# Low parts of the fp32 split moved from GpSimd to VectorE in the last two token tiles and the second feed-forward layer

## The chip, the cores and the metric

The kernel runs on one core of one Trainium2 chip. The metric is device time in microseconds, the median of several runs. The engines are PE (TensorE matmul, with PEld for its weight loads), DVE (VectorE), ACT (ScalarE), POOL (GpSimd) and SP (SyncE, which here issues all DMAs). They run side by side, each in the order of its own instruction queue, and wait for each other by semaphores.

## The reference, cut to what matters

Three stages are computed one after the other on 3072 tokens (4 batches of 768). All data are fp32.

```
# 1. linear attention with decay, 8 heads of 32, state 16, in chunks along the sequence
y = scan_attention(x, a, B, C)            # [3072 tokens, 256]
# 2. first feed-forward layer, w1 w2 w3: 256 x 768, w_out: 768 x 256
h = max(max(y @ w1, y @ w2), y @ w3)
x = h @ w_out
# 3. second feed-forward layer, w_gate w_val: 256 x 1536, w_out: 1536 x 256
out = (sigmoid(x @ w_gate) * (x @ w_val)) @ w_out
```

## The kernel before, in words

**Split in high and low parts.** Each fp32 operand of a big matmul is kept as two tiles of the faster type float32r: `hi` is a rounded copy made by ACT, `lo = value - hi` is what rounding lost. A product is three matmuls: lo times hi, hi times lo, hi times hi. So every weight block, every input operand and every gated tile needs one ACT cast and one subtraction, and a low part can't be made before its cast.

**Stages.** Tokens are cut in six tiles of 512 (t = 0 to 5). Attention chunks are computed ahead of and between the matmuls of the first layer in tiles 0 to 3. In the first layer a tile has six blocks m of 128 hidden columns. A block, called a layer step below, is 18 matmuls into three PSUM banks (tiles `u_t_m_0` to `u_t_m_2`) and 6 matmuls of the down product (tiles `o_t_0`, `o_t_1`) of the block before it. The three PSUM banks are a ring: matmuls of the next step can only write bank 1 after the bank of this step has been read.

**What is done with a step's banks** (function `most`): ACT copies bank 0 to `s` (L467), DVE takes the maximum with bank 1 (L469) and with bank 2 (L471), ACT casts `s` to `hi` (L460), and a subtraction makes `lo` (L462, in `hidden`).

**Weights of the second layer** come as raw 64-bit words in 18 pieces (`g0`, `v0`, `d0` to `g5`, `v5`, `d5`) and are decoded on the chip by `decode`: three ACT passes (L164, L169, L173), two DVE passes (L177, L182), for pieces g and v four small DVE sums (L195), ACT casts (L201), and the low parts (L204: one subtraction of 512 columns for the four blocks, and for g and v another of 384 columns for three sums). Decoding starts in tile 4, one piece in a layer step, and goes on in the second layer. `behind(k)` is a hint on order: the instruction is issued after the last eviction of a PSUM bank on ACT (k = 0) or DVE (k = 1).

**Operands of the second layer.** `operands(p)` makes seven sums and differences of two token tiles and splits each (`operand`: L431 is the ACT cast, L432 the subtraction). p = 0 is made in tiles 4 and 5, p = 1 and 2 later. The second layer computes, for each p and each j of 6 pieces, 14 products of three matmuls (L605), evicts and gates them (L609 to L619, L670), splits the gated tile (L673 on ACT, L674 on DVE) and multiplies it by the down weights (L634).

**Order.** The program is written as generators that are advanced in turns; a scheduler then orders the instructions of each engine by its own estimate of time. So the place of an instruction on its engine is set by that scheduler, under the data dependences and the `behind` hints. All DMAs are issued by SP.

Of the kernel before, what the change touches and what calls it, by code (L numbers as in the profile page):

```python
# [8 lines left out]
F32 = mybir.dt.float32  # L9
# [6 lines left out]
ALU = mybir.AluOpType  # L16
# [10 lines left out]
NTT = NT // TT  # L27
# [43 lines left out]
def scan_attention_then_ffn(ctx: ExitStack, tc: tile.TileContext, xh, ah, bch, pick, bn, w1, w2, w3,  # L71
                            wo1, wg, wv, wo2, out):
    nc = tc.nc
    act, dve, pool, pe, sp = nc.scalar, nc.vector, nc.gpsimd, nc.tensor, nc.sync
# [41 lines left out]
    def store2(wpool, tags, name):  # L116

        nb = 4 if name[0] == "d" else 7
        if len(tags) == 1:
            w = wpool.tile([128, 2, nb, 128], F32R, tag=tags[0], name=f"w_{name}")  # L120
            hi, lo = w[:, 0], w[:, 1]
        else:
            hi, lo = (wpool.tile([128, nb, 128], F32R, tag=g, name=f"w_{name}{k}")
                      for k, g in enumerate(tags))
        wt2[name] = [(hi[:, b], lo[:, b]) for b in range(nb)]
        return hi, lo
# [25 lines left out]
    def decode(raw, wpool, blocks, name):  # L152
        nb = raw.shape[1]
        second = name[0] != "a"

        def behind(k):
            return tc.issue_after(evict[k].ins) if second else ExitStack()

        f1 = raw[..., 1]
        r = stp.tile([128, DEC // 128, 128], I32, tag="r", bufs=3, name=f"r_{name}")[:, 0:nb]  # L160
        sg = sgs[len(blocks_done) % len(sgs)][:, 0:nb]
        blocks_done.append(name)
        with behind(0):
            act.activation(out=sg.bitcast(F16).rearrange("p b (n t) -> p b n t", t=2)[..., 1], in_=f1.bitcast(F32),  # L164
                           func=AF.Identity, scale=2.0 ** -112)
        if second:
            yield
        with behind(0):
            act.mul(f1.bitcast(F32), f1.bitcast(F32), 2.0 ** -112)  # L169
        if second:  # L170
            yield
        with behind(0):
            act.mul(r, raw[..., 0].bitcast(U32), 2.0 ** -29)  # L173
        yield
        t = stp.tile([128, DEC // 128, 128], I32, tag="t", bufs=2, name=f"t_{name}")[:, 0:nb]
        with behind(1):
            dve.scalar_tensor_tensor(out=t, in0=f1, scalar=3, in1=sg, op0=ALU.logical_shift_left,  # L177
                                     op1=ALU.bitwise_or)
        if second:
            yield  # L180
        with behind(1):
            dve.tensor_tensor(out=r, in0=t, in1=r, op=ALU.add)  # L182
        yield
        if second:
            hi, lo = store2(wpool, blocks, name)
            parts = [(r.bitcast(F32), slice(0, 4))]
            if name[0] != "d":
                v = r.bitcast(F32)
                q = wq[0].tile([128, 3, 128], F32, tag="q", name=f"q_{name}")
                for k, (out, x, y, op) in enumerate(((q[:, 0], v[:, 1], v[:, 3], ALU.add),  # L190
                                                     (q[:, 2], v[:, 0], v[:, 1], ALU.subtract),
                                                     (q[:, 1], q[:, 0], v[:, 0], ALU.subtract),
                                                     (v[:, 1], v[:, 2], q[:, 1], ALU.subtract))):
                    with behind(1):
                        dve.tensor_tensor(out=out, in0=x, in1=y, op=op)  # L195
                    if k % 2:
                        yield
                parts.append((q, slice(4, 7)))
            for x, at in parts:
                with behind(0):  # L200
                    act.copy(hi[:, at], x)  # L201
                yield
            for x, at in parts:
                pool.tensor_tensor(out=lo[:, at], in0=x, in1=hi[:, at].bitcast(F32), op=ALU.subtract)  # L204
            return
        w = wpool.tile([128, 2, nb, 128], F32R, tag=name, name=f"w_{name}")
        blocks += [(w[:, 0, b], w[:, 1, b]) for b in range(nb)]
        act.copy(w[:, 0], r.bitcast(F32))
        yield
        pool.tensor_tensor(out=w[:, 1], in0=r.bitcast(F32), in1=w[:, 0].bitcast(F32),  # L210
                           op=ALU.subtract)

    def weights_tick(last=True):
        if loaded and last:
            pipe.add(decode(*loaded.pop(0)))
# [179 lines left out]
    def three(ps, ks, kn, w, blk, a_hi, a_lo):  # L395

        for k in ks:
            whi, wlo = w[blk(k)]
            pe.matmul(ps, wlo, a_hi(k), start=k == 0, stop=False)  # L399
            pe.matmul(ps, whi, a_lo(k), start=False, stop=False)  # L400
            pe.matmul(ps, whi, a_hi(k), start=False, stop=k == kn - 1)  # L401
# [18 lines left out]
    def at(k, t):  # L420
        return y1[:, k, t * TT:(t + 1) * TT]
# [8 lines left out]
    def operand(i, src, eng):  # L430
        act.copy(x7[0][:, SLOT[i]], src)  # L431
        eng.tensor_tensor(out=x7[1][:, SLOT[i]], in0=src, in1=x7[0][:, SLOT[i]].bitcast(F32),  # L432
                          op=ALU.subtract)

    def operands(p):

        eng = dve if p else pool
        b11, b12, b21, b22 = (at(k, 2 * p + t) for k in range(2) for t in range(2))
        operand(1, b11, eng)
        dve.tensor_tensor(out=b12, in0=b12, in1=b11, op=ALU.subtract)  # L440
        yield
        operand(2, b21, eng)
        yield
        operand(5, b12, eng)
        yield
        dve.tensor_tensor(out=b12, in0=b22, in1=b12, op=ALU.subtract)
        operand(6, b12, eng)
        yield
        dve.tensor_tensor(out=b11, in0=b12, in1=b11, op=ALU.subtract)
        operand(7, b11, eng)  # L450
        yield
        dve.tensor_tensor(out=b21, in0=b21, in1=b12, op=ALU.subtract)
        yield
        operand(3, b22, dve)
        yield
        operand(4, b21, dve)

    def hidden(s, hl, eng):
        yield
        act.copy(hl[0], s)  # L460
        yield
        eng.tensor_tensor(out=hl[1], in0=s, in1=hl[0].bitcast(F32), op=ALU.subtract)  # L462

    def most(s, banks, hl):

        yield
        evict[0] = act.copy(s, banks[0])  # L467
        yield
        dve.tensor_tensor(out=s, in0=banks[1], in1=s, op=ALU.max)  # L469
        yield  # L470
        evict[1] = dve.tensor_tensor(out=s, in0=banks[2], in1=s, op=ALU.max)  # L471
        yield from hidden(s, hl, pool)

    chain = Pipe()

# [4 lines left out]
    def layer(t, m, w, n, stages):  # L480

        o = (t * TT) % RING
        s = tmpp.tile([128, TT], F32, tag="s", bufs=3, name=f"s{n}_{t}_{m}")
        hl = [tmpp.tile([128, TT], F32R, tag=h, name=f"{h}{n}_{t}_{m}") for h in ("hi", "lo")]
        banks = []
        for j in range(n):
            ps = psu.tile([128, TT], F32, tag="up", name=f"u{n}_{t}_{m}_{j}")
            three(ps, range(KD), KD, w, lambda k: KD * j + k,
                  lambda k: xt_hi[:, k, o:o + TT], lambda k: xt_lo[:, k, o:o + TT])
            banks.append(ps)  # L490
            if j == 0:
                chain.add(stages(s, banks, hl))
            yield hl


# [151 lines left out]
    for p in range(NTT // 2):  # L647
        for j in range(M2 // 2):
            two = {k: Product(p, j, k) for k in "gv"}
            made = {}  # L650
            if p < 2 and j == M2 // 2 - 1:
                later = operands(p + 1)
            else:
                later = None
            for u, step in enumerate(PLAN):
# [8 lines left out]
                else:  # L664
                    kind, i = step[0], int(step[1])
                    k = two[kind].multiply(i)
                    if kind == "v" and k is not None:
# [7 lines left out]
                                          op=ALU.subtract)  # L675
# [76 lines left out]
```

## Time and profile before

| | |
|---|---|
| median of 3 runs | 569.61 us (568.42 to 570.89) |
| the profiled execution | 568.34 us |
| its span from first to last instruction | 566.2 us |
| mean granted TensorE clock | 0.985 |
| busy share of the span: PE, DVE, ACT, POOL | 94%, 70%, 57%, 33% |
| POOL instructions | 206 |

The span is 2.1 us shorter than the time of the same execution. A busy share is a mean over stages that have different limits: here attention lies in the first 200 us, tiles 4 and 5 of the first layer between about 213 and 285 us, the second layer behind them.

### The profile page before, as it was taken

How to read it: one execution, taken by the hardware profiler on the slowest of the kernel's cores; microseconds unless marked ns; L12 is line 12 of the kernel's file. 1: busy time of each engine (PE TensorE's matmuls, PEld its weight loads, DVE VectorE, ACT ScalarE, POOL GpSimd, SP SyncE). 2: the span in 40 equal slices, each digit the busy share in tenths (PEclk: the TensorE clock that was granted, in tenths of full speed). 3: DMA queues.
4: the chain of work that ended last, by engine and by line, in shares of the span. 5: the costliest groups of instructions: out<-in, count | busy, mean ns of one | idle time of the engine just before them, and what ended most of it. 6: DMA issues, size and time to landing. Idle time of an engine off the chain costs nothing.

```text
span 566.2 us, 7999 instructions
## 1 busy us (share of the span) xinstructions
PE 533.4 (94%) x2885; PEld 421.3 (74%) x2885; DVE 395.4 (70%) x603; ACT 325.0 (57%) x580; POOL 189.5 (33%) x206
## 2 busy tenths in 40 slices
PE   4768899999999999998989999999999999999996
PEld 4656667677777778876867877877888887788885
DVE  3899985666876733899987897586555567555555
ACT  4787735334434233667688887566555565555553
POOL 3567956464655433488641233000000000000000
PEclk9869899999999999999999999999999999999999
DMA  7999985893996119013220000002000002000001
GB/s 244 346 264 236 242 175 113 190 178 123 194 204 124 30 37 335 1 37 113 75 75 1 1 1 2 0 0 75 0 1 0 2 1 75 0 1 0 1 1 74
DMA packets 32007, 50.52 MB, mean 89 GB/s; under 512 B 3168, under 2 KB 17888, under 8 KB 31968
## 3 DMA queue, kind: packets, MB, share of 16 engines
q1 hardware_dynamic: 31968, 50.02, 33.8%
q8 instruction: 22, 0.36, 0.3%
q14 instruction: 17, 0.14, 0.1%
HBM read 38.51 MB, written 3.25 MB: 74 GB/s over the span
## 4 chain that ended last, share of the span: by engine, by line
PE 65%; DVE 14%; ACT 7%; DMA 7%; issue 4%; POOL 1%; SPq 1%; DVEq 0%; ACTq 0%; POOLq 0%
PE o L634 14%; PE ug L605 12%; PE uv L605 12%; PE u L399 6%; PE u L400 6%; PE u L401 6%; DMA raw_a<-in_w 3%; PE o L399 2%; PE y L350 2%; PE o L400 2%; PE o L401 2%; PE s L332 1%; DVE q_v L195 1%; DVE r_v L182 1%; DMA dec<-ad 1%
## 5 line engine op out<-in xcount | busy, mean ns | idle before, releaser
L634 PE MATMUL o<-hi,w_d 128*128 128x512 f32 x288 | 97.7, 390 | 0.6 <-ACT hi L673 0.6
L399 PE MATMUL u<-xt_hi,w_a 128*128 128x512 f32 x216 | 89.5, 414 | 6.2 <-DVE s L469 3.3
L605 PE MATMUL ug<-xt_hi,w_g 128*128 128x512 f32 x252 | 91.5, 391 | 1.4 <-ACT y L609 1.4
L605 PE MATMUL uv<-xt_hi,w_v 128*128 128x512 f32 x252 | 90.5, 391 | 0.5 <-DVE s L471 0.5
L400 PE MATMUL u<-xt_lo,w_a 128*128 128x512 f32 x216 | 85.9, 398 | 1.8 <-DVE xt_lo L361 1.8
L401 PE MATMUL u<-xt_hi,w_a 128*128 128x512 f32 x216 | 85.8, 397 | 0.0
L462 POOL TENSOR_TENSOR lo<-s,hi 128x512 fp32r<-128x512 f32 x36 | 50.6, 1404 | 42.1 <-ACT hi L460 41.9
L634 PEld LDWEIGHTS o<-hi,w_d 128*128 128x128 f32 x288 | 53.9, 188 | 12.3 <-ACT hi L673 1.3
L674 DVE TENSOR_TENSOR lo<-y,hi 128x512 fp32r<-128x512 f32 x72 | 50.8, 706 | 16.8 <-ACT hi L673 15.9
L288 DVE TENSOR_TENSOR_SCAN dec<-dec,delta 128x388 f32<-128x388 f32 x64 | 57.9, 945 | 2.3 <-DMA dec<-ad 2.1
L634 PE MATMUL o<-lo,w_d 128*128 128x512 f32 x144 | 56.6, 393 | 1.8 <-DVE lo L674 1.6
L605 PEld LDWEIGHTS ug<-xt_hi,w_g 128*128 128x128 f32 x252 | 47.3, 188 | 12.9 <-ACT y L609 1.8
L605 PEld LDWEIGHTS uv<-xt_hi,w_v 128*128 128x128 f32 x252 | 47.3, 188 | 11.9 <-DVE s L471 0.9
L460 ACT CAST hi<-s 128x512 fp32r<-128x512 f32 x36 | 22.3, 620 | 58.7 <-DVE s L471 58.4
L399 PEld LDWEIGHTS u<-xt_hi,w_a 128*128 128x128 f32 x216 | 41.5, 192 | 18.6 <-DVE s L469 4.1
L605 PE MATMUL ug<-xt_lo,w_g 128*128 128x512 f32 x126 | 49.1, 390 | 0.0
L605 PE MATMUL uv<-xt_lo,w_v 128*128 128x512 f32 x126 | 49.1, 389 | 0.0
L400 PEld LDWEIGHTS u<-xt_lo,w_a 128*128 128x128 f32 x216 | 41.5, 192 | 10.0 <-DVE xt_lo L361 2.3
L673 ACT CAST hi<-y 128x512 fp32r<-128x512 f32 x72 | 44.7, 621 | 6.7 <-DVE y L670 6.7
L401 PEld LDWEIGHTS u<-xt_hi,w_a 128*128 128x128 f32 x216 | 41.3, 191 | 9.2
L670 DVE TENSOR_TENSOR y<-uv,y 128x512 f32<-128x512 f32 x36 | 24.8, 688 | 32.9 <-PE uv L605 32.9
L612 DVE TENSOR_TENSOR y<-ug,y 128x512 f32<-128x512 f32 x36 | 24.8, 689 | 26.5 <-ACT y L609 18.9
(100 smaller groups left out, 987.0 us busy)
## 6 DMA issues: line engine op xcount, KB each, us to landing
dec<-ad SPq DMA_DIRECT2D x30, 388.0 KB, 5.6
raw_a<-in_w SPq DMA_DIRECT2D x18, 256.0 KB, 6.8
bi<-parts SPq DMA_DIRECT2D x36, 128.0 KB, 6.0
cs<-parts SPq DMA_DIRECT2D x36, 96.0 KB, 6.1
xs<-in_xh SPq DMA_DIRECT2D x6, 512.0 KB, 5.2
raw_g<-in_wg SPq DMA_DIRECT2D x6, 512.0 KB, 5.0
raw_v<-in_wv SPq DMA_DIRECT2D x6, 512.0 KB, 5.9
raw_d<-in_wo SPq DMA_DIRECT2D x6, 512.0 KB, 3.7
```

Source lines behind the costliest of these rows:

```text
L288: dve.tensor_tensor_scan(out=f, data0=f, data1=delta.rearrange("p u w -> p (u w)"), initial=0.0, op0=ALU.mult, op1=ALU.add)
L399: pe.matmul(ps, wlo, a_hi(k), start=k == 0, stop=False)
L400: pe.matmul(ps, whi, a_lo(k), start=False, stop=False)
L401: pe.matmul(ps, whi, a_hi(k), start=False, stop=k == kn - 1)
L460: act.copy(hl[0], s)
L462: eng.tensor_tensor(out=hl[1], in0=s, in1=hl[0].bitcast(F32), op=ALU.subtract)
L605: pe.matmul(ps, w, x, start=new and e == 0, stop=e == 2, skip_group_check=not new)
L612: evict[1] = dve.tensor_tensor(out=self.t[k], in0=ps, in1=self.t[k], op=ALU.add)
L634: pe.matmul(acc2[t][d], w, x, start=n == 1 and e == 0, stop=n == M2 and e == 2)
L670: evict[1] = dve.tensor_tensor(out=g, in0=v, in1=g, op=ALU.mult)
L673: act.copy(hl[0], g)
L674: dve.tensor_tensor(out=hl[1], in0=g, in1=hl[0].bitcast(F32), op=ALU.subtract)
```

## The change

Three subtractions that make low parts are given to DVE instead of POOL: those of the second layer's weights (L204, with the hint to stand behind the last eviction on DVE), those of the first five operands of `operands(0)` (L432; the later ones were on DVE already), and those of the hidden tiles of the first layer in token tiles 4 and 5 (L462). From the fifth tile on POOL does no arithmetic. No DMA, no matmul and no ACT instruction is added or taken away, and POOL issues no DMA in either kernel.

```
             for x, at in parts:
-                pool.tensor_tensor(out=lo[:, at], in0=x, in1=hi[:, at].bitcast(F32), op=ALU.subtract)
+                with behind(1):
+                    dve.tensor_tensor(out=lo[:, at], in0=x, in1=hi[:, at].bitcast(F32),
+                                      op=ALU.subtract)
...
     def operands(p):
-        eng = dve if p else pool
+        eng = dve
...
-    def most(s, banks, hl):
+    def most(s, banks, hl, eng):
...
-        yield from hidden(s, hl, pool)
+        yield from hidden(s, hl, eng)
...
-                chain.add(stages(s, banks, hl))
+                chain.add(stages(s, banks, hl, dve if t > NTT - 3 else pool))
```

Lines behind the first edit have numbers higher by two in the changed kernel (L471 there is L469 here). In the rows below `s_5_0` is the hidden tile of token tile 5, block 0, and `u_5_0_1` its PSUM bank 1; `y_91` holds token tiles.

DVE between the last maximum of step 4_5 and that of step 5_0, before:

```order
L471 TENSOR_TENSOR s_4_5_2528<-u_4_5_2_2557,s_4_5_2528 128x512
L177 SCALAR_TENSOR_TENSOR t_g_2574<-raw_g_2333,sg_88 128x512
L182 ISA r_g_2541<-t_g_2574,r_g_2541 128x1024
L195 TENSOR_TENSOR q_g_2600<-r_g_2541 128x128 x2
L195 TENSOR_TENSOR q_g_2600<-q_g_2600,r_g_2541 128x128
L195 TENSOR_TENSOR r_g_2541<-r_g_2541,q_g_2600 128x128
L446 TENSOR_TENSOR y_91<-y_91 128x512
L449 TENSOR_TENSOR y_91<-y_91 128x512
L469 TENSOR_TENSOR s_5_0_2576<-u_5_0_1_2590,s_5_0_2576 128x512
L452 TENSOR_TENSOR y_91<-y_91 128x512
L471 TENSOR_TENSOR s_5_0_2576<-u_5_0_2_2604,s_5_0_2576 128x512
```

The same place on DVE now (without the first maximum, which is still ahead of it):

```order
L177 SCALAR_TENSOR_TENSOR t_g_2574<-raw_g_2333,sg_88 128x512
L434 TENSOR_TENSOR xt_lo<-y_91,xt_hi 128x512 x2
L182 ISA r_g_2541<-t_g_2574,r_g_2541 128x1024
L464 TENSOR_TENSOR lo_4_5_2530<-s_4_5_2528,hi_4_5_2529 128x512
L448 TENSOR_TENSOR y_91<-y_91 128x512
L195 TENSOR_TENSOR q_g_2600<-r_g_2541 128x128 x2
L471 TENSOR_TENSOR s_5_0_2576<-u_5_0_1_2590,s_5_0_2576 128x512
L451 TENSOR_TENSOR y_91<-y_91 128x512
L454 TENSOR_TENSOR y_91<-y_91 128x512
L195 TENSOR_TENSOR q_g_2600<-q_g_2600,r_g_2541 128x128
L434 TENSOR_TENSOR xt_lo<-y_91,xt_hi 128x512
L473 TENSOR_TENSOR s_5_0_2576<-u_5_0_2_2604,s_5_0_2576 128x512
```

Four low parts (three operands, one hidden tile) stand in this stretch that stood on POOL, and the maximum of bank 1 is now ahead of part of the sums of piece g.

ACT at the passage from the first layer to the second, before (`ug`, `uv` are product banks of the second layer, `o_5` the down product of tile 5):

```order
L607 COPY uv_0_1_2931<-uv_0_0_2927 128x512
L619 ACT_TABLE_LOAD
L619 ACTIVATE y_91<-ug_0_1_2922 128x512
L201 CAST w_v_2936<-q_v_2937 128x384
L201 CAST w_v_2936<-r_v_2856 128x512
L609 COPY y_91<-ug_0_0_2918 128x512
L418 COPY y_91<-o_5_0_2669 128x512
L418 COPY y_91<-o_5_1_2670 128x512
L609 COPY sv_0_1_2973<-uv_0_0_2927 128x512
L673 CAST hi_0_0_2966<-y_91 128x512
```

And now:

```order
L609 COPY uv_0_1_2931<-uv_0_0_2927 128x512
L621 ACT_TABLE_LOAD
L621 ACTIVATE y_91<-ug_0_1_2922 128x512
L611 COPY y_91<-ug_0_0_2918 128x512
L611 COPY sv_0_1_2973<-uv_0_0_2927 128x512
L420 COPY y_91<-o_5_0_2669 128x512
L675 CAST hi_0_0_2966<-y_91 128x512
L201 CAST w_v_2936<-q_v_2937 128x384
L420 COPY y_91<-o_5_1_2670 128x512
L201 CAST w_v_2936<-r_v_2856 128x512
```

The first copy of a gate bank (L609 before) has moved ahead of the two casts of a weight piece.

## Rows read from the trace of the kernel before

**Rows 1.** Busy time of each engine in four stretches; columns in the first line.

```profile
core 0: us, PE busy (x) PEld busy (x) DVE busy (x) ACT busy (x) POOL busy (x), PEclk, DMA share, GB/s
200.00:229.30 29.30, 29.30 (x163) 23.61 (x162) 9.96 (x14) 10.89 (x19) 8.64 (x7) 1.00 0.50 180
229.30:250.00 20.70, 20.70 (x93) 17.15 (x92) 19.18 (x25) 15.45 (x27) 15.01 (x11) 1.00 0.00 0
250.00:297.00 47.00, 41.79 (x179) 32.52 (x178) 43.20 (x59) 33.03 (x60) 30.30 (x22) 1.00 0.28 90
297.00:352.00 55.00, 54.10 (x235) 43.47 (x234) 46.48 (x77) 46.38 (x86) 16.69 (x12) 1.00 0.00 1
```

**Rows 2.** Timeline of PE, matmuls with a wait: start, duration, [idle before, releaser].

```profile
254.55 0.50 PE L399 MATMUL u<-xt_hi,w_a 128*128 128x512 f32 x1 [1.33 <-DVE s L469]
...
261.66 0.50 PE L399 MATMUL u<-xt_hi,w_a 128*128 128x512 f32 x1 [1.96 <-DVE s L469]
...
284.45 0.50 PE L605 MATMUL uv<-xt_hi,w_v 128*128 128x512 f32 x1 [0.50 <-DVE s L471]
...
291.74 0.50 PE L605 MATMUL ug<-xt_hi,w_g 128*128 128x512 f32 x1 [1.39 <-ACT y L609]
```

**Rows 3.** Timeline of DVE, 239 to 299 us.

```profile
239.54 0.69 DVE L469 TENSOR_TENSOR s<-u,s 128x512 f32<-128x512 f32 x1
...
240.94 1.80 DVE L177 SCALAR_TENSOR_TENSOR t_d<-raw_d,sg 128x512 int32<-128x512 int32 x1
242.88 1.58 DVE L182 CUSTOM_DVE_ANT_0 r_d<-t_d,r_d 128x1024 uint16<-128x1024 uint16 x1
...
260.93 0.68 DVE L469 TENSOR_TENSOR s<-u,s 128x512 f32<-128x512 f32 x1
...
281.98 0.49 DVE L195 TENSOR_TENSOR q_g<-r_g 128x128 f32<-128x128 f32 x2
282.39 0.28 DVE L195 TENSOR_TENSOR q_g<-q_g,r_g 128x128 f32<-128x128 f32 x1
...
297.60 0.68 DVE L612 TENSOR_TENSOR y<-ug,y 128x512 f32<-128x512 f32 x1
298.20 0.68 DVE L182 CUSTOM_DVE_ANT_0 r_d<-t_d,r_d 128x1024 uint16<-128x1024 uint16 x1
```

**Rows 4.** Timeline of POOL beside them.

```profile
240.90 1.29 POOL L204 TENSOR_TENSOR w_v<-r_v,w_v 128x512 fp32r<-128x512 f32 x1
242.15 1.75 POOL L462 TENSOR_TENSOR lo<-s,hi 128x512 fp32r<-128x512 f32 x1
...
300.17 1.30 POOL L204 TENSOR_TENSOR w_d<-r_d,w_d 128x512 fp32r<-128x512 f32 x1 [7.16 <-ACT w_d L201]
```

**Rows 5.** DVE busy of single lines in 229.3 to 297: L177, L182, L195, L432.

```profile
229.30:297.00 67.70, 13.90 (x10) 1.00 0.19 63
...
229.30:297.00 67.70, 13.93 (x10) 1.00 0.19 63
...
229.30:297.00 67.70, 12.89 (x32) 1.00 0.19 63
...
229.30:297.00 67.70, 3.20 (x2) 1.00 0.19 63
```

**Rows 6.** POOL busy of single lines in 229.3 to 297: L462, L204, L432.

```profile
229.30:297.00 67.70, 16.59 (x10) 1.00 0.19 63
...
229.30:297.00 67.70, 22.23 (x18) 1.00 0.19 63
...
229.30:297.00 67.70, 6.89 (x4) 1.00 0.19 63
```

**Rows 7.** Timeline of ACT at the passage to the second layer.

```profile
290.18 0.51 ACT L201 CAST w_v<-q_v 128x384 fp32r<-128x384 f32 x1 [1.64 <-DVE q_v L195]
...
291.11 0.58 ACT L609 COPY y<-ug 128x512 f32<-128x512 f32 x1
```

**Rows 8.** Groups of DVE in 297 to 352: count, busy us, mean ns of one.

```profile
L674 DVE TENSOR_TENSOR lo<-y,hi 128x512 fp32r<-128x512 f32 x15 | 11.6, 772 | 3.6 <-ACT hi L673 3.6
L670 DVE TENSOR_TENSOR y<-sv,y 128x512 f32<-128x512 f32 x8 | 7.3, 913 | 1.2 <-ACT y L614 0.8
```

## The prediction

> **What bounds the kernel now.** PE is busy for most of the span, so I first asked where PE waits in the part that the change touches, then who is late there, and then why. The busy time by stretches gives the first answer [rows 1]: PE has no gap from 200 to 250 us, loses 47.00 - 41.79 = 5.21 us between 250 and 297 us, and 0.90 us between 297 and 352 us. TensorE's granted clock is 1.00 (of 2.4 GHz) in each of these stretches, so a gap is a wait and nothing else. The timeline of PE names the waits [rows 2]: 1.33 and 1.96 us for the maximum L469, 0.50 us for L471, 1.39 us for the copy L609 on ACT, together 5.18 of the 5.21 us. Three of the four wait for DVE directly. The fourth waits for ACT, where L609 at 291.11 us stood behind the cast of a weight piece that had waited 1.64 us for DVE's L195 [rows 7]. So DVE is what is late. In 229.3 to 297 us (67.7 us: tile 4 from step 2 on, tile 5 and the passage to the second layer) it is busy 19.18 + 43.20 = 62.4 us, as much as PE with 62.5 us [rows 1].
>
> Why DVE is so full is seen by laying POOL beside it. L182 takes 0.68 us at 298.20 us, while POOL is idle (its instruction at 300.17 us ends an idle time of 7.16 us) [rows 3, 4]. At 242.88 us the same instruction takes 1.58 us, and POOL is at work on L462 from 242.15 to 243.90 us. DVE ends at 244.46 us, 0.56 us after POOL. The L177 ahead of it ends at 242.74 us, 0.55 us after POOL's L204 ended at 242.19 us [rows 3, 4]. POOL's L462 in turn takes 1.75 us where L204 took 1.29 us. The two engines take turns: such a DVE instruction does its own 0.55 to 0.6 us of work once POOL's instruction has ended, and its duration includes the wait. L469 at 239.54 us, which reads one operand from PSUM, takes 0.69 us [rows 3] although POOL works through most of this stretch [rows 1].
>
> **The change part by part.**
>
> *What leaves POOL.* In 229.3 to 297 us it is 10 + 18 + 4 = 32 subtractions with 16.59 + 22.23 + 6.89 = 45.7 us of POOL time [rows 6]. Eight of the 18 of L204 have 384 columns (four g and four v pieces), the other 24 have 512. Twelve more follow between 297 and 352 us, and three (two hidden tiles, one operand) lie before 229.3 us, where DVE is busy 9.96 of 29.30 us and PE has no gap [rows 1]; these three I cost at nothing, and without that cover they would be 3 x 0.6 = 1.8 us.
>
> *What it costs on DVE.* In a row of instructions without waits DVE starts one of 512 columns every 0.60 us (297.60 and 298.20 us) [rows 3]. Two of 128 columns take 0.49 us together and one alone 0.28 us [rows 3], so a step from start to start is 0.2 us. Between these, 384 columns are by my estimate about 0.47 us. Sum: 24 x 0.60 + 8 x 0.47 = 18.2 us.
>
> *What DVE gets back.* Three lines that meet POOL [rows 5]: L177 took 13.90 us for 10, where 10 x 0.69 would be 6.9, so 7.0 us; L182 13.93 us, again 7.0 us; L195 12.89 us for 32, where a piece without POOL is 0.49 + 2 x 0.28 = 1.06 us [rows 3] and eight pieces 8.5 us, so 4.4 us. L432 took 3.20 us for two against 1.3, so 1.9 us. Together 20.3 us; L440, L449 and L452 (one each here) are left out. DVE's load becomes 62.4 + 18.2 - 20.3 = 60.3 us, against 62.5 us that PE needs. So it fits with about 2 us to spare, where today it fills the stretch and runs late.
>
> The Trainium skill, Perfetto Trace Analysis, section Optimizing Scalar/DVE Operations, speaks against the change with one sentence and for it with the next: with a saturated DVE, offloading work to another engine, even GpSimd, may make sense, but the two share an SBUF read port, so moving operations between them might not help. By its first half the sum would be the 18.2 us more on DVE with nothing given back (the second rival); the durations in this trace bear out the second half.
>
> *Whether it fits where PE waits.* The two long waits grow between the maxima L469 of steps 4_4 (239.54 us) and 5_1 (260.93 us): DVE took 21.4 us [rows 3] for three layer steps that PE does in 3 x 24 x 20.70 / 93 = 16.0 us [rows 1]. In the new order DVE has 23 instructions of 512 columns, 5 of 128 and 2 of 384 between them (counted; the middle of it is shown with the change), 13.8 + 1.0 + 0.9 = 15.7 us. That is a hair under PE's pace. A dependent neighbour costs a tenth more (0.69 instead of 0.60 us), so it may run up to a microsecond late. The ring of banks gives room for that: after bank 1 of a step is full, 18 matmuls pass (18 x 0.223 = 4.0 us) before PE needs it, 3.3 us more than L469 takes. I therefore take both waits, and the 0.50 us behind them, as gone: 3.8 us. The other bound is that one of the long ones stays (2 us).
>
> *What waits behind the new instructions.* Each low part now stands in DVE's queue and waits for its ACT cast, with the next maxima queued behind it and PE behind them. ACT is busy 48.5 of 67.7 us [rows 1], and the new order puts one to four other DVE instructions between a maximum and the low part of the same tile, 0.6 us each, against 0.6 us of a cast. I take 0; the other bound is in the first rival.
>
> *The passage to the second layer.* L609 has moved ahead of the two casts, and DVE is no longer late, so the 1.39 us should mostly go. But ACT's table load, the evictions of `o_5` and the first gated tile still meet there. I keep half, 0.7 us; the bounds are 0 and 1.4.
>
> *The second layer, 297 to 352 us.* At most 12 x 0.6 = 7.2 us come to DVE, and what meets POOL there is less: 15 x (0.772 - 0.69) + 8 x (0.913 - 0.69) = 3.0 us from two groups alone [rows 8]. DVE goes from 46.5 to at most 50.7 us, where PE needs 54.1 us [rows 1]. That is hidden by PE's work, but with little room. I take no change of the 0.90 us of waits; bounds -0.9 and +2 us. Behind 352 us POOL has no work in either kernel, and nothing changes but the start. SP's queue and its DMAs keep their order.
>
> **Sum**, against the profiled execution's own 568.34 us: minus 5.2 us of waits, plus 0.7 us that stay, is 563.8 us, a gain of 4.5 us or 0.8%. The median of the runs is 1.27 us above that execution; scaled to it, 569.61 x 563.8 / 568.34 = 565.0 us.
>
> **The rivals.** First: low parts block DVE's queue. If the cast is late, a maximum behind the low part is late by the same time, and with three such steps in a row the ring's 3.3 us are used up. For it: ACT also waits for DVE (the 1.64 us) [rows 7], so lateness on one comes back on the other. Against it: the new order interleaves them. Price: the two long waits return, 3.3 us, and the gain is 1.2 to 1.9 us: about 568.0 us by the median.
>
> Second, slower: DVE becomes the bound. If the long durations of L177, L182 and L195 come only in part from POOL, DVE gains 18.2 us of work and gets back less than I counted. The stretch is 67.7 us long, so it gets longer once less than 62.4 + 18.2 - 67.7 = 12.9 us of the 20.3 are returned. With 8 us returned it is 4.9 us longer: 574.5 us by the median. Against it: the ends fall 0.55 us after POOL's in both pairs, and 0.68 us stands beside 1.58 us for one and the same operation.
>
> Third: the second layer pays. In 297 to 352 us each of the 12 subtractions waits for a cast with evictions behind it; if PE's waits there grow from 0.9 to 2.9 us, the gain is 2.5 us: 567.1 us.
>
> **How the numbers follow.** The forecast has 0.60 (a gain of 3 us or more), the first rival 0.18, the third 0.13, the slower one 0.09. About 0.5% (2.8 us) is what a measurement of this kernel can tell from no change. The third rival lies at that bound, so I give half of it to faster: 0.66 faster, 0.24 same (the first rival and the rest of the third), 0.10 slower. The likeliest time is 565.0 us. The lower end is all 6.1 us of waits gone and a microsecond of scatter between runs: 562.5 us. The upper end takes in the first and third rival with the same scatter, 569.2 us, and leaves out the slower one and a little more.
>
> **What would show it.** Right: L177 and L182 at 0.68 us each in tiles 4 and 5, no POOL row after about 215 us, DVE less busy in 229 to 297 us, and no wait of PE for L469 (L471 in the new numbering) above half a microsecond. Wrong: DVE idle in front of the low parts for a cast, with a PE wait behind (first rival); DVE durations still above 1 us (second); new PE waits for hi or lo of gated tiles behind 290 us (third).

## The result and the profile after

Five runs of each kernel gave 562.13 us (562.01 to 562.54) after the change and 569.38 us (568.42 to 570.89) before it: a ratio of 0.987, with an interval of 0.985 to 0.989. The change gains 7.25 us where 4.5 us were forecast. The profiled execution took 562.02 us with a span of 560.2 us.

Busy time of each engine in the changed kernel, in the same four stretches as [rows 1]:

```profile
core 0: us, PE busy (x) PEld busy (x) DVE busy (x) ACT busy (x) POOL busy (x), PEclk, DMA share, GB/s
200.00:229.30 29.30, 29.30 (x163) 23.59 (x162) 11.31 (x18) 10.60 (x19) 5.25 (x5) 1.00 0.49 180
229.30:250.00 20.70, 20.70 (x93) 17.15 (x92) 17.86 (x36) 15.34 (x28) 0.00 (x0) 1.00 0.00 0
250.00:297.00 47.00, 46.98 (x208) 38.58 (x207) 44.26 (x90) 39.08 (x71) 0.00 (x0) 1.00 0.29 90
297.00:352.00 55.00, 54.99 (x242) 44.73 (x241) 44.86 (x84) 43.65 (x81) 0.00 (x0) 1.00 0.00 1
```

PE's gaps are gone: 0.02 us where 5.21 us were missing, 0.01 where it was 0.90. In 250 to 297 us PE does 208 matmuls; before it did 179 [rows 1]. POOL has nothing to do from 229.3 us on. DVE is about as full as it was (17.86 + 44.26 = 62.1 us against 62.4 [rows 1]), but with more work inside. What it does now, by groups of instructions from 229.3 to 297 us (mean ns of one behind the busy time, then the idle time ahead of them and who ended it):

```profile
line engine op names shapes xcount | busy us, mean ns | idle before us <-releasers
L473 DVE TENSOR_TENSOR s<-u,s 128x512 f32<-128x512 f32 x10 | 6.9, 692 | 2.0 <-PE u L403 1.9
L471 DVE TENSOR_TENSOR s<-u,s 128x512 f32<-128x512 f32 x10 | 6.9, 691 | 3.4 <-PE u L403 3.1 <-ACT w_g L201 0.3
L464 DVE TENSOR_TENSOR lo<-s,hi 128x512 fp32r<-128x512 f32 x10 | 6.9, 691 | 0.5 <-ACT hi L462 0.5
...
L182 DVE CUSTOM_DVE_ANT_0 r_g<-t_g,r_g 128x1024 uint16<-128x1024 uint16 x4 | 2.8, 693 | 0.1
...
L177 DVE SCALAR_TENSOR_TENSOR t_d<-raw_d,sg 128x512 int32<-128x512 int32 x4 | 2.8, 688 | 0.0
```

L182 takes 693 ns and L177 688 ns; in [rows 5] ten of each took 13.9 us, 1.39 us apiece. The maxima L471 (L469 before) wait 3.1 us for PE: DVE is now early, and PE no longer waits for it. The ten moved low parts of hidden tiles (L464) made DVE wait 0.5 us in all for their casts. The timeline of DVE at the place of [rows 3], start and duration first:

```profile
239.53 0.69 DVE L471 TENSOR_TENSOR s<-u,s 128x512 f32<-128x512 f32 x1
...
240.82 0.69 DVE L473 TENSOR_TENSOR s<-u,s 128x512 f32<-128x512 f32 x1 [0.40 <-PE u L403]
241.43 0.68 DVE L177 SCALAR_TENSOR_TENSOR t_d<-raw_d,sg 128x512 int32<-128x512 int32 x1
242.02 0.56 DVE L205 TENSOR_TENSOR w_v<-q_v,w_v 128x384 fp32r<-128x384 f32 x1
242.49 0.69 DVE L205 TENSOR_TENSOR w_v<-r_v,w_v 128x512 fp32r<-128x512 f32 x1
243.09 0.69 DVE L182 CUSTOM_DVE_ANT_0 r_d<-t_d,r_d 128x1024 uint16<-128x1024 uint16 x1
243.69 0.69 DVE L464 TENSOR_TENSOR lo<-s,hi 128x512 fp32r<-128x512 f32 x1
...
256.55 0.69 DVE L471 TENSOR_TENSOR s<-u,s 128x512 f32<-128x512 f32 x1
```

L177 and L182 stood here with 1.80 and 1.58 us [rows 3]. Their time now holds three subtractions besides: from 241.43 to 244.38 us DVE does five instructions, where the two alone took from 240.94 to 244.46 us. At 384 columns the next instruction starts 0.47 us later, as estimated. The first and the last row are the maxima of steps 4_4 and 5_1: 17.0 us apart, 21.4 before [rows 3].

A fixed stretch holds more work now than before, since PE is further on at its end. The same 269 matmuls (they begin at 229.49 us in the kernel before and at 230.65 us now), columns as above:

```profile
229.49:297.19 67.70, 62.49 (x269) 49.68 (x268) 62.38 (x82) 48.67 (x87) 45.31 (x32) 1.00 0.19 63
...
230.65:291.39 60.74, 60.74 (x269) 50.30 (x268) 55.86 (x114) 48.91 (x87) 0.00 (x0) 1.00 0.22 70
```

For this work DVE is busy for 55.9 us instead of 62.4 us, although it has 32 instructions more. The chain of work that ended last is, on the page of the changed kernel:

```profile
PE 80%; DMA 8%; DVE 7%; ACT 2%; issue 1%; SPq 1%; DVEq 0%; ACTq 0%
```

Four fifths of it are PE's own work; DVE has 7% of it.

**A measure without scatter.** The kernels below reach tile 4 at 215.0 to 217.5 us in their traces, one of them at 224.2 us, although the order on PE and ACT up to there is the same in all but the last three of the table; the time behind the last matmul differs by about a microsecond as well. For comparing traces I therefore take the time from one matmul of tile 4, `first`, to the start of the last matmul of the program; below it is called the *part*. In the part the granted clock is 1.00 in every trace but one (twin_read). The timelines of PE, before and after:

```profile
216.11 0.39 PE L644 MATMUL first<-xt_hi,w_a 128*128 128x512 f32 x1
...
252.83 0.39 PE L401 MATMUL o<-hi,w_a 128*128 128x512 f32 x1
...
254.89 0.39 PE L400 MATMUL u<-xt_lo,w_a 128*128 128x512 f32 x1
...
561.94 0.40 PE L634 MATMUL o<-hi,w_d 128*128 128x512 f32 x1
```

```profile
217.27 0.39 PE L646 MATMUL first<-xt_hi,w_a 128*128 128x512 f32 x1
...
555.04 0.39 PE L636 MATMUL o<-hi,w_d 128*128 128x512 f32 x1
```

The part went from 561.94 - 216.11 = 345.83 us to 555.04 - 217.27 = 337.77 us: 8.06 us gained. The profiled execution of after started it 1.16 us later and took about 0.9 us longer behind it, so its span is only 6.0 us shorter.

### The profile page after: what moved, and what is told of

The parts are those of the page before. It is cut to its first block, busy times and chain, and to the rows that moved or that the text cites. A ratio compares the mean times of both kernels' runs of the same rounds, so it can differ in the third digit from the quotient of the medians.

```text
span 560.2 us, 7934 instructions
## 1 busy us (share of the span) xinstructions
PE 539.3 (96%) x2885; PEld 428.7 (77%) x2885; DVE 391.0 (70%) x650; ACT 325.7 (58%) x580; POOL 123.7 (22%) x159
## 4 chain that ended last, share of the span: by engine, by line
PE 80%; DMA 8%; DVE 7%; ACT 2%; issue 1%; SPq 1%; DVEq 0%; ACTq 0%
PE o L636 17%; PE ug L607 15%; PE uv L607 15%; PE u L401 8%; PE u L402 7%; PE u L403 7%; DMA raw_a<-in_w 3%; PE o L401 3%; PE o L402 3%; PE o L403 3%; DMA dec<-ad 2%; PE y L352 2%; DVE dec L290 1%; PE s L334 1%; DMA cs<-parts 1%
## 5 line engine op out<-in xcount | busy, mean ns | idle before, releaser
L676 DVE TENSOR_TENSOR lo<-y,hi 128x512 fp32r<-128x512 f32 x72 | 49.6, 688 | 16.3 <-ACT hi L675 15.3
L462 ACT CAST hi<-s 128x512 fp32r<-128x512 f32 x36 | 22.3, 620 | 56.3 <-DVE s L473 55.8
L611 ACT COPY sv<-uv 128x512 f32<-128x512 f32 x36 | 21.1, 586 | 34.6 <-PE uv L607 34.5
```

What stands on the lines that cost most here:

```text
L611: evict[0] = act.copy(self.temp(1 if i == 6 else 2), ps)
L676: dve.tensor_tensor(out=hl[1], in0=g, in1=hl[0].bitcast(F32), op=ALU.subtract)
```

## The experiments

The theory: POOL and DVE take turns wherever both read SBUF, so DVE gets time back when POOL stops reading, and PE's waits for DVE go. A first rival: the gain comes from the new order of instructions, or from a shorter way of a low part that DVE makes at once, and what POOL does is no matter. A second: DVE gets time back in proportion to POOL's busy time, whatever POOL does. All ratios are against the kernel before on the same chip.

| kernel | median us | ratio (interval) | part us |
|---|---|---|---|
| before | 569.38 | 1 | 345.83 |
| after | 562.13 | 0.987 (0.985 to 0.989) | 337.77 |
| hidden_only | 563.94 | 0.991 (0.988 to 0.994) | 340.77 |
| weights_only | 567.44 | 0.997 (0.995 to 0.998) | 342.99 |
| operands_only | 566.0 | 0.995 (0.993 to 0.997) | 343.79 |
| hidden_operands | 563.52 | 0.991 (0.988 to 0.993) | 339.57 |
| hidden_weights | 561.64 | 0.986 (0.983 to 0.990) | 338.13 |
| twin_read | 583.1 | 1.024 (1.021 to 1.026) | 359.71 |
| twin_write | 564.57 | 0.992 (0.990 to 0.994) | 341.26 |
| twin_pin | 562.27 | 0.988 (0.985 to 0.990) | 339.47 |
| pool_write | 560.67 | 0.984 (0.982 to 0.986) | 336.90 |
| hidden_from3 | 561.95 | 0.987 (0.985 to 0.989) | 337.84 |
| all_hidden | 560.29 | 0.985 (0.983 to 0.987) | 337.80 |
| all_low | 565.52 | 0.994 (0.991 to 0.997) | 337.87 |

Not all came out as expected in the texts below. twin_read was slower than its range; twin_write and hidden_operands were 1.6 and 1.5 us slower than expected, and operands_only gained 1 us more. hidden_only fell into the range of its rival, and weights_only between those of theory and rival. The others lie within 0.6 us of a stated range.

**POOL reads again, with nothing depending on it.** The changed kernel, and beside each moved low part a subtraction of 384 columns on POOL into a tile that nobody reads:

```
+    def twin(x, h):
...
+            o, x, h = scratch, x[:, 0:384], h[:, 0:384]
+        pool.tensor_tensor(out=o, in0=x, in1=h.bitcast(F32), op=ALU.subtract)
...
                     dve.tensor_tensor(out=lo[:, at], in0=x, in1=hi[:, at].bitcast(F32),
                                       op=ALU.subtract)
+                twin(x, hi[:, at])
...
```

The operands and the hidden tiles get the same call.

> The changed kernel, and beside each low part that DVE makes, POOL makes most of it once more (384 of 512 columns, or of 384) into a scratch tile that nobody reads. Output unchanged. Theory (DVE and POOL take turns, and PE waited for the DVE time lost so): L177, L182 and L195 take well over their 0.69 and 0.29 us again wherever POOL reads, DVE now loses turns with its own low parts too, PE waits for L471 and L473 come back, 568 to 580 us. Rival (the new order on ACT and DVE made the gain, or the low parts' shorter way): the order is nearly that of the changed kernel and the low parts are still made on DVE, so 562 to 563 us and no such waits.

**POOL writes as long, and reads one column.** The same, with another `twin`:

```
+    def twin(x, h):
...
+        pool.tensor_tensor(out=scratch[:, 0:1], in0=x[:, 0:1], in1=h[:, 0:1].bitcast(F32), op=ALU.subtract)
+        for _ in range(2):
+            pool.memset(scratch, 0.0)
```

> As twin_read, with the same order on PE, DVE and ACT, but POOL's twin reads one column and then fills the scratch tile twice (memset, nothing read). Output unchanged. If any POOL instruction makes DVE wait: as slow as twin_read in proportion to POOL's busy time, 566 us or more. If only POOL instructions that read SBUF do: DVE durations at 0.69 and 0.29 us and 562 to 563 us. I expect the second.

Busy time from 229.3 to 297 us, first of the kernel whose POOL reads (583.1 us), then of the one whose POOL writes (564.57 us); columns as above:

```profile
229.30:250.00 20.70, 19.90 (x88) 16.16 (x87) 20.30 (x30) 13.39 (x24) 10.95 (x9) 1.00 0.00 0
250.00:297.00 47.00, 36.80 (x144) 26.76 (x143) 46.80 (x66) 26.81 (x47) 26.43 (x21) 0.96 0.26 79
```

```profile
229.30:250.00 20.70, 20.70 (x93) 17.15 (x92) 17.86 (x35) 15.36 (x28) 10.13 (x27) 1.00 0.00 0
250.00:297.00 47.00, 45.88 (x199) 36.62 (x198) 42.57 (x86) 37.46 (x68) 28.99 (x72) 1.00 0.28 90
```

POOL is busy for 37.4 us in the one and 39.1 us in the other, in nearly the same order of instructions on PE, DVE and ACT, and the times are 18.5 us apart. With reads, DVE has no free time left (20.30 of 20.70, 46.80 of 47.00 us) and PE does 144 matmuls where it does 199 with fills. (TensorE's granted clock is 0.96 in this stretch: from 284.7 to 288.1 us, behind the wait of 3.50 us shown below, it is 1.2 GHz, and matmuls start 0.43 instead of 0.23 us apart. That is 1.6 us of the 18.5.) In the first one DVE and POOL at one place, in the timeline:

```profile
242.18 1.50 DVE L214 TENSOR_TENSOR w_v<-r_v,w_v 128x512 fp32r<-128x512 f32 x1
243.61 1.51 DVE L191 CUSTOM_DVE_ANT_0 r_d<-t_d,r_d 128x1024 uint16<-128x1024 uint16 x1
...
242.05 1.09 POOL L148 TENSOR_TENSOR scratch<-s,hi 128x384 bf16<-128x384 f32 x1 [3.42 <-ACT hi L474]
243.22 1.35 POOL L148 TENSOR_TENSOR scratch<-r_v,w_v 128x384 bf16<-128x384 f32 x1
```

POOL ends at 243.14 and 244.57 us, DVE at 243.68 and 245.12 us: each time 0.54 to 0.55 us later, as in [rows 3, 4]. The kernel before shows the same throughout: from 216 to 352 us, 36 DVE instructions with both inputs in SBUF start while POOL is at work, and every one ends 0.55 us behind POOL's instruction (0.14 to 0.15 us where it has 128 columns); the 79 that start while POOL is idle take 0.70 us at most. Where POOL only writes, each group of L191 and L186 has a mean of 0.68 to 0.69 us. So the proportional rival falls, and POOL's reads are what holds DVE up. The run also shows what the second rival of the prediction would have looked like: a DVE that takes up the stretch, and PE waits for its low parts, as in this row of PE's timeline:

```profile
283.74 0.50 PE L412 MATMUL o<-lo,w_a 128*128 128x512 f32 x1 [3.50 <-DVE lo L476]
```

One low part that came late left PE idle for 3.5 us here. The Trainium skill, SBUF — State Buffer, section SBUF: two separate sides, says of such turns that a DVE instruction with two SBUF inputs and a GpSimd instruction share a port pair as a lock for a whole instruction, but only where the GpSimd instruction reads SBUF; this pair of runs agrees.

**The order of before, and POOL writes only.** The kernel before, in which POOL reads one column and then fills each of these low parts with zeros, in two instructions, instead of subtracting (this leaves the low parts out of the result):

```
+    def low(out, x, h):
...
+        pool.tensor_tensor(out=o[:, 0:1], in0=x[:, 0:1], in1=h[:, 0:1].bitcast(F32), op=ALU.subtract)
+        for _ in range(2):
+            pool.memset(out.bitcast(F32), 0.0)
...
-                pool.tensor_tensor(out=lo[:, at], in0=x, in1=hi[:, at].bitcast(F32), op=ALU.subtract)
+                low(lo[:, at], x, hi[:, at])
...
```

> The kernel before, with its order on PE and ACT and (but for a few swaps) on DVE, where POOL makes the same 47 low parts in about the same time without reading them: one column is read, then the tile is filled with zero twice. The low parts are left out of the result so, all waits for them stay. Theory (DVE waits for POOL instructions that read): L177, L182 and L195 at 0.69 and 0.29 us, PE's waits for L469 go, 561 to 564 us although nothing was moved to DVE. Rival (the new order made the gain, or the low parts' shorter way): order and way are those of before, so 567 to 570 us.

Its busy time in three stretches:

```profile
229.30:250.00 20.70, 20.70 (x93) 17.15 (x92) 13.74 (x27) 15.31 (x28) 13.16 (x32) 1.00 0.00 1
250.00:297.00 47.00, 47.00 (x209) 38.80 (x208) 32.81 (x67) 39.12 (x71) 27.92 (x68) 1.00 0.28 90
297.00:352.00 55.00, 55.00 (x245) 45.52 (x244) 39.70 (x74) 43.57 (x82) 13.74 (x33) 1.00 0.00 1
```

Nothing has moved to DVE, PE's order is that of before, and POOL is busy for 13.16 + 27.92 = 41.1 us, yet PE has no wait. DVE is busy for 46.6 us instead of 62.4 [rows 1]. At the place of [rows 3, 4] the timelines of DVE and POOL read:

```profile
241.61 0.68 DVE L186 SCALAR_TENSOR_TENSOR t_d<-raw_d,sg 128x512 int32<-128x512 int32 x1
242.43 0.69 DVE L191 CUSTOM_DVE_ANT_0 r_d<-t_d,r_d 128x1024 uint16<-128x1024 uint16 x1
...
241.10 0.19 POOL L146 TENSOR_TENSOR w_v<-q_v,w_v 128x1 fp32r<-128x1 f32 x1 [1.72 <-ACT w_v L210]
241.35 0.42 POOL L148 MEMSET w_v<- 128x384 f32 x1
241.73 0.62 POOL L146 TENSOR_TENSOR w_v<-r_v,w_v 128x1 fp32r<-128x1 f32 x1
242.28 0.88 POOL L148 MEMSET w_v<- 128x384 f32 x2
```

The custom instruction L191 runs in 0.69 us beside two fills that last from 242.28 to 243.16 us. The read of one column takes 0.19 us at 241.10 us, but 0.62 us at 241.73 us, where it ends at 242.35 us, just behind DVE's L186 (242.29 us): here POOL waited its turn. This settles it against the rival of the order: with the order of before and POOL's reads gone the gain is there (560.67 us). At the passage the copy of the gate bank stands behind the two casts of a weight piece as before (casts at 284.18 and 284.58 us, copy at 285.11 us), and PE has no wait there either, so that wait did not go because of the new order on ACT.

**The three groups alone.** Each is the changed kernel with two of the three edits undone; the first has only the hidden tiles on DVE:

```
-        eng = dve
+        eng = dve if p else pool
...
-                with behind(1):
-                    dve.tensor_tensor(out=lo[:, at], in0=x, in1=hi[:, at].bitcast(F32),
-                                      op=ALU.subtract)
+                pool.tensor_tensor(out=lo[:, at], in0=x, in1=hi[:, at].bitcast(F32), op=ALU.subtract)
```

> The kernel before with only the hidden tiles' low parts of token tiles 4 and 5 on DVE (12 of 47). Theory: about a third of POOL's time in the crowded stretch goes (16.6 of 45.7 us), and about a third of the gain comes, 566 to 567.5 us. Rival (low parts' way is what counted): these are the only low parts that PE needs at once, so most of the gain, 562 to 564 us.

The second has only the weights on DVE, the third only the operands. Both have the hidden tiles back on POOL, and one of the two edits above:

```
-                chain.add(stages(s, banks, hl, dve if t > NTT - 3 else pool))
+                chain.add(stages(s, banks, hl, pool))
```

> The kernel before with only the weights' low parts on DVE (30 of 47). Theory: half of POOL's time in the crowded stretch goes (22.2 of 45.7 us) and all of it in the second layer, so half of the gain or somewhat more, 564 to 566 us. Rival (low parts' way): no PE wait named such a weight, so 568 to 570 us.

> The kernel before with only the five operand low parts on DVE. Four of them (6.9 us of POOL time) lie between 246 and 259 us, just where the two long waits of PE (1.33 and 1.96 us) grow. Theory: these waits shrink by about half, 567 to 568.5 us, and the waits at the passage to the second layer stay. If part gains add up to the whole, hidden, weights and operands alone give about 7 us in sum.

The part gains 5.06, 2.84 and 2.04 us. The lines L177, L182 and L195 took 18.4 us more than their own work in the kernel before (13.90 + 13.93 + 12.89 - 22.3 us [rows 5]); by the same count it is 8.9, 3.5 and 15.6 us in these three, and none in the kernel after. So the hidden tiles gain more than their share of POOL's time, and the weights, which give most back in these three lines, gain less. The hidden tiles' 563.94 us is the figure of the rival, but its reason is not borne out: no wait of PE in the kernel before, from 216 us on, names a low part that POOL made. What differs is how full DVE is over the same 269 matmuls as above (hidden tiles, weights, operands):

```profile
229.98:292.46 62.48, 61.60 (x269) 50.01 (x268) 56.98 (x92) 48.33 (x87) 29.75 (x22) 1.00 0.21 68
...
230.12:295.79 65.67, 62.21 (x269) 49.76 (x268) 62.77 (x100) 48.60 (x88) 22.45 (x14) 1.00 0.20 65
...
229.50:295.22 65.72, 61.96 (x269) 49.76 (x268) 61.07 (x86) 48.47 (x87) 39.06 (x28) 1.00 0.21 65
```

DVE was busy for 62.4 us before. The hidden tiles alone take 5.4 us off it and the operands 1.3 us. The weights take off nothing; why they still gain 2.0 us here is not shown. With only the weights moved, from 229.3 to 297 us, the moved ones themselves wait for POOL (groups of DVE):

```profile
L205 DVE TENSOR_TENSOR w_v<-r_v,w_v 128x512 fp32r<-128x512 f32 x4 | 4.9, 1235 | 0.0
L205 DVE TENSOR_TENSOR w_g<-q_g,w_g 128x384 fp32r<-128x384 f32 x4 | 4.4, 1102 | 0.0
```

These take 1.24 and 1.10 us instead of 0.69 and 0.56. Two of the waits that PE keeps in that kernel, in its timeline:

```profile
256.49 0.50 PE L401 MATMUL u<-xt_hi,w_a 128*128 128x512 f32 x1 [1.27 <-DVE s L473]
261.48 0.50 PE L401 MATMUL u<-xt_hi,w_a 128*128 128x512 f32 x1 [0.61 <-DVE s L471]
```

**Two groups together.** The changed kernel with the weights back on POOL, and with the operands back on POOL:

```
-                with behind(1):
-                    dve.tensor_tensor(out=lo[:, at], in0=x, in1=hi[:, at].bitcast(F32),
-                                      op=ALU.subtract)
+                pool.tensor_tensor(out=lo[:, at], in0=x, in1=hi[:, at].bitcast(F32), op=ALU.subtract)
```

> The kernel before with hidden tiles and operands moved (17 of 47). Alone they gave, from the matmul that begins the second layer's banks (at 216 us) to the last matmul, 5.1 and 2.0 us of the whole change's 8.1. If parts add up: 7.1 us, 562 us. If what counts is that DVE's lateness stays under what the ring of banks allows: both long waits and the one at the passage are gone already, 7 to 8 us, 562 us as well, and the last 1 us, in the second layer, stays.

```
-        eng = dve
+        eng = dve if p else pool
```

> The kernel before with hidden tiles and weights moved (42 of 47), operands left on POOL. If parts add up: 5.1 + 2.8 = 7.9 us of the 8.1, 562 us. If the four operand instructions on POOL, next to each other where DVE is fullest, still make it late: one wait for a maximum between 250 and 262 us stays, about 1.5 us, 563 to 564 us.

They gain 6.26 and 7.70 us of the part. (The profiled execution of the second took 569.29 us, since it lost 7 us ahead of the part; its median in the table is that of the other three.) The sum of the three alone is 9.9 us, more than 8.06: the parts don't add. That fits a PE that waits only once DVE's lateness exceeds what the ring of banks gives, which is argued, not shown. With the weights back on POOL the waits of the second layer stay, 0.32, 0.57 and 0.34 us; with the operands back there is none from 250 to 352 us. Hidden tiles and weights carry the gain, and the operands add 0.4 us.

**The twin that reads one column and nothing more.** The kernel with POOL's writes was still 3.5 us of the part slower than after, so I took its fills away:

```
-        for _ in range(2):
-            pool.memset(scratch, 0.0)
```

> twin_write without the two fills: POOL only reads one column beside each low part. Shows what of the 3.5 us that twin_write is slower than the changed kernel (from 216 us on) comes from the fills: if fills cost nothing, it is the same as twin_write, 564 to 565 us (order and the one-column reads are to blame); if the fills hold DVE up, 562 us.

The part is 339.47 us, about half-way between 341.26 and 337.77. What is left are PE waits of 0.28 and 0.72 us in the second layer for an eviction on ACT, as with the fills (0.48, 0.19, 0.45 and 0.73 us there). DVE's L186 and L191 (L184 and L189 without the fills) take 0.68 to 0.69 us in both kernels, so the fills did not lengthen them. The order changed with the edit too (36 places on DVE, 45 on PE, 28 on ACT), so how much of the 3.5 us the fills cost and how much the order stays open.

**Further in the same direction.** The hidden tiles from tile 3 on, of all tiles, and also the low parts of the first layer's weights:

```
-                chain.add(stages(s, banks, hl, dve if t > NTT - 3 else pool))
+                chain.add(stages(s, banks, hl, dve if t > NTT - 4 else pool))
```

> The changed kernel, with the hidden tiles of token tile 3 moved too (6 more low parts). Between 180 and 213 us PE has a single wait of 0.43 us and DVE is half idle, so by the theory nothing is to be had: 562 us, within 0.5 us of the changed kernel. A rival (less POOL is better everywhere) would give 0.5 to 1 us.

```
+                chain.add(stages(s, banks, hl, dve))
```

> The changed kernel, with the hidden tiles' low parts of all token tiles on DVE (24 more). In tiles 0 to 2 POOL also works for attention and DVE is 70 to 85% busy. Theory: DVE takes 24 x 0.6 = 14 us more and gets back only where it met these POOL instructions; PE's waits there are about 5 us in all. 560.5 to 564 us, likeliest the same as the changed kernel.

```
+                chain.add(stages(s, banks, hl, dve))
...
-        pool.tensor_tensor(out=w[:, 1], in0=r.bitcast(F32), in1=w[:, 0].bitcast(F32),
+        dve.tensor_tensor(out=w[:, 1], in0=r.bitcast(F32), in1=w[:, 0].bitcast(F32),
```

> As all_hidden, with the low parts of the first layer's weights on DVE as well (12 more, between 30 and 110 us, where DVE is busy 85% and decodes these weights itself). Theory: each meets DVE's own two decode instructions on POOL today, so about even: 560 to 565 us.

All three change only what lies ahead of the part, and have the part of the changed kernel within 0.1 us, so only the whole time can tell. The first two can't be told from the changed kernel by it (the second has the lowest median of the kernels that compute everything, 560.29 us, with an interval that overlaps). The third is 3.4 us slower than the changed kernel by the medians, and its runs spread from 562.21 to 570.08 us. In its trace, of an execution of 569.35 us, the part starts at 225.36 us instead of 217.27 and ACT waits 6.3 us for the transfer of a weight piece. Such a loss is also in the trace of hidden_weights (224.24 us, a wait of 3.6 us), where nothing ahead of the part was edited, so how much of it the edit made is not shown.

## Why the prediction came out as it did

**The mechanism held.** That DVE and POOL take turns, that DVE's long instructions shrink to 0.69 us, and that PE's waits for DVE go with them is what the runs show: with POOL's reads back PE waits again (583.1 us), with POOL's reads gone and the order of before it does not (560.67 us). DVE's load was forecast as 60.3 us. The fixed stretch shows 62.1 us, but with eleven instructions more than were forecast for it; for the same matmuls it is 55.9 us. So DVE got back 62.4 + 18.2 - 55.9 = 24.7 us, not 20.3. The prediction counted L177 and L182 with 0.69 us each, where in a row one starts every 0.60 us (20 x 0.09 = 1.8 us), and left out L440, L449 and L452 (1.35, 1.39 and 1.16 us before, 2.1 us more than three times 0.60). The forecast time does not hang on this, since PE was taken as the bound either way.

**The step that failed is the size of the sum, in three places.** The forecast was 5.2 - 0.7 = 4.5 us, measured on the part are 8.06.

- *The waits were priced by the idle column, and they cost more.* The idle time that went is 5.21 - 0.02 + 0.90 - 0.01 = 6.08 us, and the part got 8.06 us shorter, 2.0 us more. The rows above show why. A matmul lasts 0.39 us in the trace, but the next one normally starts 0.227 us behind its start (the median of the part), so idle time begins to count 0.16 us late. The matmul behind the wait lasts 0.50 us [rows 2], and the next one starts 0.34 us behind it. From 252.83 to 254.89 us are two steps, 2.06 us instead of 0.45: 1.60 us lost where the row says 1.33. Six waits (the four of [rows 2] and 0.56 and 0.19 us in the second layer) make 6 x 0.27 = 1.6 us more than their idle time, 7.57 us from start to start. Of the 8.06 us this leaves 0.5 us: 0.2 us are late starts with less than 0.15 us of idle time (1.07 us before, 0.87 us now, from 250 to 352 us), and 0.25 us are spread over starts less than 0.25 us apart.
- *The passage to the second layer kept nothing* of the 0.7 us that I left there; 0 was a bound of that term. The copy of the gate bank, L609 in [rows 7], now starts with no wait in ACT's timeline:

```profile
283.50 0.60 ACT L621 ACTIVATE y<-ug 128x512 f32<-128x512 f32 x1
283.99 0.59 ACT L611 COPY y<-ug 128x512 f32<-128x512 f32 x1
```

- *The second layer, taken as no change, gave its 0.89 us too.* This was the lower bound of that term. It belongs to the weights on POOL: with them alone back, the waits there return.

4.5 + 0.7 + 0.89 + 2.0 = 8.1 us. My lower end, 562.5 us, took all 6.1 us of idle time as the most that could go, and a microsecond of scatter; the measured 562.13 us lies 0.4 us below it, since that idle time was not the most.

**The rivals.** The casts did not block DVE's queue: 0.5 us for ten low parts. DVE did not become the bound, and the second layer did not pay. What I had counted for DVE's passing (23 instructions of 512 columns between two maxima, 15.7 us) was 17.0 us from maximum to maximum, 1.0 us of waits for PE included, against 16.0 us that PE needs: the microsecond of lateness that I had allowed for, and the ring took it. A dependent neighbour costs more than the 0.69 us of the prediction: L471 starts 0.79 us behind L469 (240.33 and 239.54 us in the kernel before).

## What to carry to other kernels

Before giving an engine's work to GpSimd, look whether VectorE's instructions that read two SBUF tiles end some half a microsecond after GpSimd's: then an offloaded subtraction can cost VectorE in waiting more than doing it would cost. Here VectorE took 32 subtractions back and was busy for 55.9 instead of 62.4 us over the same matmuls. An experiment in which GpSimd stays as busy but only writes separates the two causes in one run. Price a wait of PE from start to start of matmuls, not from the idle column: here 6.1 us of idle time went with 8.1 us of the part.

## What the runs showed of the hardware

Fills on POOL leave DVE's two-input instructions alone (0.69 us beside fills from 242.28 to 243.16 us), while POOL's reads hold them up until 0.55 us after POOL's end (0.15 us for 128 columns). The turns go both ways: POOL's read of a single column lasted 0.62 instead of 0.19 us and ended 0.06 us behind DVE's L186. A subtraction of 512 columns, 1.29 us on POOL [rows 4], takes 0.69 us on DVE and lets the next one start after 0.60 us.
